# Splitting the first convolution chunk over all four quadrants of the matmul array, with the tap sums formed in PSUM and a weight copied in column halves

## The chip, the cores and the metric

The kernel runs on one core of a Trainium2 chip. A core has a matmul engine (TensorE, PE in the profile) that reads SBUF and writes PSUM, a vector engine (VectorE, DVE), a scalar engine (ScalarE, ACT), a GpSimd engine (POOL, here the issuer of casting loads), a SyncE queue (SP, here the issuer of stores and transposing transfers) and 16 DMA engines. The metric is the device time of one execution in microseconds; lower is better.

## The reference

Two layers in a row. The first is a causal convolution over the sequence, 7 taps, with one softmax-normalised set of taps for each of 8 heads (24 channels each). The second is a two-layer network with a leaky ReLU.

```
x: (8, 4096, 192) f32   weight: (8, 7)   w_in: (192, 2048)   w_out: (2048, 192)
w    = softmax(weight, axis=-1)          # with + 1e-9 in the denominator
conv[b, s, ch] = sum_k w[head(ch), k] * x_padded[b, s + k, ch]    # 6 zeros in front
h    = conv.reshape(32768, 192) @ w_in
out  = maximum(0.01 * h, h) @ w_out
```

## The kernel before

**Tiling.** Channels are cut into 3 chunks (`NCH`) of 64. Two batch rows share the 128 partitions: row e (0 or 1) of a pair has partitions 64e to 64e+63. `xt[pair]` holds x transposed (channels on partitions, tokens along the free side) in bf16, `yt[block]` the convolved block of 512 tokens (`ST`). The first two blocks are cut into halves of 256 tokens, so that `groups` begins with four groups of 256 and goes on with whole blocks. For each group the loop at the end of the kernel runs steps of first-layer matmuls (`mm1`, line 494: `ph` <- `w_in`, `yt`), a leaky ReLU on ScalarE (line 501: `g` <- `ph`) and second-layer matmuls of the group before (lines 511 and 574). The convolution of a later group is made by VectorE (lines 226 and 232: one instruction per chunk and tap).

**The opening.** Before any of that runs, the first group needs its convolution quickly, and there TensorE does it: for each chunk c, part p and tap k it multiplies 256 tokens, shifted by k, with a 64x64 diagonal matrix `diag[c][:, p, k, :]` (line 257, `acc` <- `xt`, `diag`), adding the 14 products in PSUM. The taps are split in two bf16 parts (p = 0 the rounded exponential, p = 1 the remainder), so that no precision is lost; a third part is used only for the sum. Matmuls with 64 rows and 64 columns take one quadrant of the array each: e gives the row half, the output's partitions the column half. With `cross` the output of row e goes to the other half of the partitions, so that a crossed chunk and a straight one use all four quadrants; its evacuation crosses back.

**Order in the opening.** Everything is written out by hand, and each engine takes its instructions in program order.

- The exponentials of the weights (ScalarE, line 370) are split into three bf16 parts on VectorE (lines 377 to 380, `w9p`), and three 48-column matmuls with the 0/1 matrix `sel` spread parts 0 and 1 over the channels (`select`, line 394); VectorE copies them to SBUF as `whm` (line 407).
- TensorE runs warm-up matmuls (line 358) between these pieces. Block 0's first 256 tokens are transposed by matmuls against `ident` (line 179), with a `select` of part 2 in the middle, and copied to `xt` by ScalarE (line 199).
- The diagonals: VectorE makes planes of 7 taps (`diag_wide`, line 413: chunk 0 both parts, chunk 2 part 0, four taps of chunk 1 part 1, chunk 2 part 1), ScalarE single taps (`diag_each`, line 421: the other ten of chunk 1).
- VectorE adds the parts (line 441 `wml`), forms the denominator (line 443) and its reciprocal `rsum` (line 447). Then it copies `w_in[0]` within SBUF (`spread_down` line 320, `spread_up` line 323): each half of the first-layer weights is loaded once and needed on both partition halves.
- TensorE: chunk 0 part 0 alone (7 steps of 2 matmuls), chunk 0 part 1 with chunk 2 part 0 (7 steps of 4), chunk 1 part 1 with chunk 2 part 1 (7 of 4), chunk 1 part 0 alone (7 of 2).
- Evacuations, scaled by `rsum`: chunk 0 on ScalarE (line 452), chunk 2 half on ScalarE and half on VectorE (line 276), chunk 1 on ScalarE.
- TensorE transposes the next 256 tokens from `x_rows[1]` (line 188), which POOL's queue loads; VectorE copies them to `xt` (line 199) and forms `wk`, the normalised taps for its own convolutions (lines 469 and 470).
- The main loop's group 0: chunks in the order 0, 2, 1 (`FIRST`). Behind its first two units TensorE starts the convolution of group 1, chunks 0 and 2 (line 257 again), in three cuts, while VectorE makes chunk 1 of it (seven taps, lines 226 and 232) with the copies of `w_in[1]` behind the third tap. Units 0 and 1 of `mm1` read columns 0 to 511 of `w_in[0]`, units 2 and 3 columns 512 to 1023, units 4 to 7 the same of `w_in[1]`.

PSUM: pool `po` has four one-bank buffers for the transposes and the accumulators, pool `ph` two buffers of two banks; `wa` (warm-ups) and `wps` (the `select` outputs) have the first two turns of `ph`, the first-layer outputs the next.

## Time and profile before

| | us |
|---|---|
| median of 4 runs (lowest, highest) | 681.78 (681.32, 682.85) |
| the profiled execution | 681.65 |
| its span, first to last instruction | 679.9 |
| TensorE busy | 675.9 (99%) |
| VectorE busy | 480.8 (71%) |
| ScalarE busy | 518.7 (76%) |
| first-layer matmuls, line 494, busy | 377.1 |
| second-layer matmuls, line 574, busy | 339.9 |
| convolution matmuls, line 257 (140 of them), busy | 5.5 |
| copies of `w_in`, lines 320 and 323 (4), busy | 2.3 |

Times in a timeline are microseconds from the start of the span; a row merges instructions of one kind that follow each other, "start, length, engine, line, operation, output<-inputs, shape, count", and in brackets the idle time before it with what ended it. Matmuls are pipelined: a row's length holds the latency of its last instruction, so the step from one to the next is found from the count and the mean. A matmul of a pair or a four of quadrants starts a few ns after its neighbour.

### The profile page before, as it was taken

How to read it: one execution, taken by the hardware profiler on the slowest of the kernel's cores; microseconds unless marked ns; L12 is line 12 of the kernel's file. 1: busy time of each engine (PE TensorE's matmuls, PEld its weight loads, DVE VectorE, ACT ScalarE, POOL GpSimd, SP SyncE). 2: the span in 40 equal slices, each digit the busy share in tenths (PEclk: the TensorE clock that was granted, in tenths of full speed). 3: DMA queues.
4: the chain of work that ended last, by engine and by line, in shares of the span. 5: the costliest groups of instructions: out<-in, count | busy, mean ns of one | idle time of the engine just before them, and what ended most of it. 6: DMA issues, size and time to landing. Idle time of an engine off the chain costs nothing.

```text
span 679.9 us, 27088 instructions
## 1 busy us (share of the span) xinstructions
PE 675.9 (99%) x12444; PEld 447.3 (66%) x12444; DVE 480.8 (71%) x811; ACT 518.7 (76%) x608; POOL 146.8 (22%) x205
## 2 busy tenths in 40 slices
PE   9999999999999999999999999999999999999998
PEld 6997666666666666666666666666666666666667
DVE  7989468766768666778667687667786676876612
ACT  7899777777777778777777877778777777777781
POOL 7455210222201222202222202222022220000000
PEclk9999999999999999999999999999999999999999
DMA  9998745656737557456556556667375573321123
GB/s 150 93 111 110 58 79 88 81 63 73 95 72 96 71 56 88 81 86 87 64 65 92 87 84 76 58 83 94 73 90 66 59 95 73 72 56 35 32 50 94
DMA packets 213826, 53.27 MB, mean 78 GB/s; under 512 B 209232, under 2 KB 213328, under 8 KB 213712
## 3 DMA queue, kind: packets, MB, share of 16 engines
q0 software_dynamic: 98752, 13.97, 30.4%
q1 hardware_dynamic: 114944, 37.57, 28.0%
q8 instruction: 97, 1.59, 1.0%
q14 instruction: 17, 0.14, 0.1%
q10 hardware_dynamic: 16, 0.00, 0.0%
HBM read 28.31 MB, written 25.17 MB: 79 GB/s over the span
## 4 chain that ended last, share of the span: by engine, by line
PE 99%; DVE 0%; issue 0%
PE ph L494 49%; PE acc L574 44%; PE po L511 5%; PE acc L257 1%; PE warm L358 1%; PE ptr L188 0%; PE ptr L179 0%; DVE o_sb L622 0%; PE warm L394 0%; PE wps L394 0%
## 5 line engine op out<-in xcount | busy, mean ns | idle before, releaser
L501 ACT ACTIVATE g<-ph 128x1024 bf16<-128x1024 f32 x512 | 496.6, 1021 | 140.3 <-PE ph L494 140.1
L232 DVE SCALAR_TENSOR_TENSOR yt<-xt,wk,yt 128x512 bf16<-128x512 bf16 (+1 forms) x582 | 380.3, 716 | 0.2
L494 PE MATMUL ph<-yt,w_in 64*64 64x512 bf16 (+2 forms) x6048 | 377.1, 369 | 0.0
L574 PE MATMUL acc<-g,w_out 64*64 64x512 bf16 x5568 | 339.9, 376 | 0.0
L494 PEld LDWEIGHTS <-w_in 64*64 64x64 bf16 (+1 forms) x6048 | 229.6, 131 | 102.8 <-issue 0.8
L574 PEld LDWEIGHTS <-w_out 64*64 64x64 bf16 x5568 | 178.2, 118 | 118.8
L99 POOL DMA_DIRECT2D x_bf<-in_x_dram x180 | 134.2, 774 | 410.6 <-DMA xt<-x_bf 408.0
L596 DVE STREAM_TRANSPOSE o_t<-acc 128x512 f32<-128x512 f32 x87 | 72.9, 875 | 181.6 <-PE acc L574 181.6
L511 PE MATMUL po<-w_out,g 64*128 64x192 bf16 (+1 forms) x640 | 36.8, 243 | 0.0
L511 PEld LDWEIGHTS <-g 64*128 64x128 bf16 (+1 forms) x640 | 32.6, 95 | 3.2 <-issue 0.4
L226 DVE TENSOR_SCALAR yt<-xt,wk 128x512 bf16<-128x512 bf16 (+1 forms) x97 | 28.7, 320 | 3.5 <-ACT g L501 3.3
L584 ACT COPY junk<-junk 128x1 f32<-128x1 f32 x58 | 11.1, 191 | 4.1
L622 DVE COPY o_sb<-po 128x192 f32<-128x192 f32 x8 | 2.8, 356 | 6.8 <-PE po L511 4.2
L257 PE MATMUL acc<-xt,diag 64*64 64x256 bf16 x140 | 5.5, 275 | 0.0
L622 ACT COPY o_sb<-po 128x192 f32<-128x192 f32 x16 | 5.1, 323 | 0.3
L257 PEld LDWEIGHTS <-diag 64*64 64x64 bf16 x140 | 4.4, 107 | 1.4 <-DVE diag L413 0.7
L358 PE MATMUL warm<-const-bfloat16-1.0 128*128 128x512 bf16 (+3 forms) x12 | 4.3, 514 | 0.8 <-PEq L734 0.8
L152 POOL DMA_DIRECT2D x_half<-in_x_dram x6 | 4.6, 773 | 1.1 <-DMA w_in<-in_moe_w_in_dram 1.0
L358 PEld LDWEIGHTS <-const-bfloat16-1.0 128*128 128x128 bf16 x12 | 1.5, 138 | 2.5 <-issue 2.5
L148 POOL DMA_DIRECT2D x_rows<-in_x_dram x4 | 2.9, 742 | 0.0
L413 DVE TENSOR_TENSOR diag<-ident,whm 128x448 bf16<-128x448 bf16 (+1 forms) x5 | 2.6, 578 | 0.0
L421 ACT ACTIVATE diag<-ident,whm 128x64 bf16<-128x64 bf16 x10 | 2.5, 335 | 0.0
(47 smaller groups left out, 24.0 us busy)
## 6 DMA issues: line engine op xcount, KB each, us to landing
out_dram<-o_t SPq DMA_DIRECT2D x116, 192.0 KB, 4.6
x_bf<-in_x_dram POOLq DMA_DIRECT2D x180, 64.0 KB, 3.3
out_dram<-o_sb SPq DMA_DIRECT2D x8, 192.0 KB, 3.0
xt<-x_bf SPq DMA_TRANSPOSE x90, 3.9
w_out<-in_moe_w_out_dram POOLq DMA_DIRECT2D x2, 384.0 KB, 8.3
out_dram<-o_sb SPq DMA_DIRECT2D x8, 96.0 KB, 1.9
w_in<-in_moe_w_in_dram POOLq DMA_DIRECT2D x2, 256.0 KB, 5.3
x_nat<-in_x_dram SPq DMA_DIRECT2D x2, 192.0 KB, 2.6
```

The lines of the kernel that those rows point to most:

```text
L99: ins = nc.gpsimd.dma_start(out=t[:, c, :, e, :], in_=src[2 * rp + e, :, :, c * CH : (c + 1) * CH],)
L226: lambda s=src, d=dst, c=c: nc.vector.tensor_scalar_mul(d, s, wk[:, c, 0:1])
L232: lambda s=src, d=dst, c=c, k=k: nc.vector.scalar_tensor_tensor(out=d, in0=s, scalar=wk[:, c, k : k + 1], in1=d, op0=mybir.AluOpType.mult, ...
L257: lambda k=k, p=p, a=a, ps=ps, to=to, acc=accs[e * apart]: nc.tensor.matmul(out=acc[to, :T], lhsT=diag[c][ps, p, k, :], rhs=xt[0][ps, c, a ...
L358: nc.tensor.matmul(out=wa[:, 0, 0:cols], lhsT=ones[:, 0:128], rhs=ones[:, 0:cols], start=True, stop=True,)
L494: nc.tensor.matmul(out=ph[m : m + M, e, i * T : (i + 1) * T], lhsT=w_in_of(f, e, c, m, m + M), rhs=y[ps, c, t0 : t0 + T], start=(c == chun ...
L501: act = nc.scalar.activation(out=g[blk][:, nf * u : nf * (u + 1), :, t0 : t0 + T], in_=ph.rearrange("p e (i t) -> p i e t", i=nf), func=my ...
L511: return nc.tensor.matmul(out=po[m], lhsT=g[b][ps, fc, e, s * 128 : (s + 1) * 128], rhs=w_out[ps, fc, :], start=start, stop=stop,)
L574: ins = nc.tensor.matmul(out=acc2[gi, r][e * CH : (e + 1) * CH, 0:T], lhsT=w_out_of(ps, fc, r), rhs=g[b][ps, fc, e, t0 : t0 + T], start=fi ...
L584: seal = nc.scalar.copy(out=junk, in_=junk)
L596: nc.vector.transpose(out=osb[gi, 0][:, 0 : T // GB, :, r], in_=acc2.pop((gi, r))[:, 0:T].rearrange("p (j k) -> p j k", k=GB),)
L622: ins = copy(out=o_sb[:, n % 2, :], in_=po.pop(n))
```

## The change

- Chunk 0 (`pe_conv_quads`): the 256 tokens are cut in two halves of 128. For each part and tap four matmuls run: the first half of the tokens straight into `acc0`, the second half crossed into the second bank of `wps`. That is 56 matmuls of 128 columns where there were 28 of 256. The first half is evacuated by ScalarE, the second by two VectorE instructions that cross back (64 partitions x 128).
- Chunks 1 and 2 now run together, 14 steps of four. Chunk 1's taps have the order `late`: ScalarE's three of part 1, VectorE's four of part 1, then part 0.
- The sum of the tap parts moves from VectorE to PSUM: `select` adds four parts (three and a constant 1e-9 for the denominator) in twelve 48-column matmuls behind the first transposes, in place of three in the middle of them and of a 512-column warm-up; a 192-column warm-up takes the place in the middle. VectorE forms the reciprocal and `wk` directly from PSUM, ahead of the copies.
- The copies of `w_in` are cut by column halves (`spread(n, h)`). For `w_in[0]` the first half stands behind chunk 0's evacuation and ahead of chunk 2's, the second behind the transposes of the next 256 tokens and ahead of their copies to `xt`. For `w_in[1]` the halves stand around VectorE's fourth tap.

```diff
--- before.py
+++ after.py
@@ -236,7 +236,7 @@
                 )
         return jobs
 
-    def pe_conv_jobs(grp, c, parts=(0, 1), cross=False, apart=False):
+    def pe_conv_jobs(grp, c, taps=None, cross=False, apart=False):
 
 
 
@@ -246,22 +246,22 @@
             for i in range(2 if apart else 1)
         ]
         jobs = []
-        for p in parts:
-            for k in range(K):
-                a = BASE + k + blk * ST + t0
-                both = []
-                for e in range(2):
-                    ps = slice(e * CH, (e + 1) * CH)
-                    to = slice((e ^ cross) * CH, ((e ^ cross) + 1) * CH)
-                    both.append(
-                        lambda k=k, p=p, a=a, ps=ps, to=to, acc=accs[e * apart]: nc.tensor.matmul(
-                            out=acc[to, :T], lhsT=diag[c][ps, p, k, :],
-                            rhs=xt[0][ps, c, a : a + T],
-                            start=(k == 0 and p == parts[0]),
-                            stop=(k == K - 1 and p == parts[1]),
-                        )
+        taps = taps or [(p, k) for p in range(2) for k in range(K)]
+        for p, k in taps:
+            a = BASE + k + blk * ST + t0
+            both = []
+            for e in range(2):
+                ps = slice(e * CH, (e + 1) * CH)
+                to = slice((e ^ cross) * CH, ((e ^ cross) + 1) * CH)
+                both.append(
+                    lambda k=k, p=p, a=a, ps=ps, to=to, acc=accs[e * apart]: nc.tensor.matmul(
+                        out=acc[to, :T], lhsT=diag[c][ps, p, k, :],
+                        rhs=xt[0][ps, c, a : a + T],
+                        start=((p, k) == taps[0]),
+                        stop=((p, k) == taps[-1]),
                     )
-                jobs.append(both)
+                )
+            jobs.append(both)
 
         def evac(*scale):
             if blk not in yt:
@@ -277,6 +277,43 @@
 
         return jobs, evac
 
+    def pe_conv_quads(grp, c, other):
+
+
+        blk, t0, T = grp
+        n = T // 2
+        accs = [psum_o.tile([128, ST], FP32, name="acc0", tag="po"), other]
+        jobs = []
+        for p in range(2):
+            for k in range(K):
+                a = BASE + k + blk * ST + t0
+                four = []
+                for h in range(2):
+                    for e in range(2):
+                        ps = slice(e * CH, (e + 1) * CH)
+                        to = slice((e ^ h) * CH, ((e ^ h) + 1) * CH)
+                        four.append(
+                            lambda k=k, p=p, a=a + h * n, ps=ps, to=to, acc=accs[h]: nc.tensor.matmul(
+                                out=acc[to, :n], lhsT=diag[c][ps, p, k, :],
+                                rhs=xt[0][ps, c, a : a + n],
+                                start=(k == 0 and p == 0),
+                                stop=(k == K - 1 and p == 1),
+                            )
+                        )
+                jobs.append(four)
+
+        def evac(straight, crossed):
+            if blk not in yt:
+                yt[blk] = yt_pool.tile([128, NCH, ST], BF16, name="yt")
+            y = yt[blk][:, c, t0 : t0 + T]
+            straight(y[:, 0:n], accs[0][:, :n], rsum[:, c, :])
+            for e in range(2):
+                ps = slice(e * CH, (e + 1) * CH)
+                frm = slice((1 - e) * CH, (2 - e) * CH)
+                crossed(y[ps, n:T], accs[1][frm, :n], rsum[frm, c, :])
+
+        return jobs, evac
+
     def run(*lists):
         for slots in zip_longest(*lists, fillvalue=()):
             for both in slots:
@@ -291,8 +328,9 @@
     ones = nc.const_aps.tensor(1.0, [128, ST], BF16)
     junk = const_pool.tile([128, 1], FP32)
     nc.vector.memset(junk, 0.0)
-    w9p = const_pool.tile([128, 3, K + 1], BF16, name="w9p")
+    w9p = const_pool.tile([128, 4, K + 1], BF16, name="w9p")
     nc.vector.memset(w9p, 0.0)
+    nc.vector.memset(w9p[:, 3, K:], 1e-9)
 
     sel = const_pool.tile([128, NCH, 2, CH], BF16, name="sel")
     nc.gpsimd.memset(sel[:, :, 0, :], 1.0)
@@ -316,11 +354,12 @@
             in_=moe_w_in[rows : rows + ps[1], n * WF : (n + 1) * WF],
         )
 
-    def spread_down(n):
-        nc.vector.tensor_copy(out=w_in[n][0:CH, 1, :], in_=w_in[n][CH:128, 0, :])
-
-    def spread_up(n):
-        nc.vector.tensor_copy(out=w_in[n][CH:128, 1:3, :], in_=w_in[n][0:CH, 0:3:2, :])
+    def spread(n, h):
+        cols = slice(h * WF // 2, (h + 1) * WF // 2)
+        nc.vector.tensor_copy(
+            out=w_in[n][CH:128, 1:3, cols], in_=w_in[n][0:CH, 0:3:2, cols]
+        )
+        nc.vector.tensor_copy(out=w_in[n][0:CH, 1, cols], in_=w_in[n][CH:128, 0, cols])
 
     def w_in_of(f, e, c, m0, m1):
         n, f = divmod(f, NFC // NPW)
@@ -385,17 +424,19 @@
     warm(3, 128)
     wps = psum_h.tile([128, 2, ST], FP32, name="wps", tag="ph")
     wps_hm = wps[:, 0, 0 : NCH * FILL].rearrange("p (c r q k) -> p c r q k", c=NCH, q=2, k=K + 1)
-    wps_l = wa[:, 1, 0 : NCH * FILL].rearrange("p (c r q k) -> p c r q k", c=NCH, q=1, k=K + 1)
-
-    def select(out, parts):
-        q = parts.stop - parts.start
-        r = FILL // (q * (K + 1))
+    wsum = wa[:, 1, 0 : NCH * FILL].rearrange("p (c r q k) -> p c r q k", c=NCH, q=1, k=K + 1)
+
+    def select(out, *parts):
         for c in range(NCH):
-            nc.tensor.matmul(
-                out=out[:, c], lhsT=sel[:, c].rearrange("p e k -> p (e k)"),
-                rhs=w9p[:, None, parts, :].to_broadcast([128, r, q, K + 1]),
-                start=True, stop=True,
-            )
+            for i, part in enumerate(parts):
+                q = part.stop - part.start
+                nc.tensor.matmul(
+                    out=out[:, c], lhsT=sel[:, c].rearrange("p e k -> p (e k)"),
+                    rhs=w9p[:, None, part, :].to_broadcast(
+                        [128, FILL // (q * (K + 1)), q, K + 1]
+                    ),
+                    start=(i == 0), stop=(i == len(parts) - 1),
+                )
 
     select(wps_hm, slice(0, 2))
     wps_hm = wps_hm[:, :, 0]
@@ -425,9 +466,9 @@
 
 
     warm(1, 192)
-    transpose_first(0, lambda: select(wps_l, slice(2, 3)))
-    wps_l = wps_l[:, :, 0, 0]
-    warm(1, ST)
+    transpose_first(0, lambda: warm(1, 192))
+    select(wsum, *(slice(i, i + 1) for i in range(4)))
+    wsum = wsum[:, :, 0, 0]
     warm(1, 384)
     evac_first(0, nc.scalar.copy, nc.scalar.copy)
     for p in range(2):
@@ -437,37 +478,29 @@
     diag_wide(2, 1, K)
     diag_each(1, 1, range(VK, K))
     diag_each(1, 0, range(K))
-    wml = const_pool.tile([128, NCH, K + 1], FP32, name="wml")
-    nc.vector.tensor_add(wml, wps_l, whm[:, :, 1])
     rsum = const_pool.tile([128, NCH, 1], FP32)
-    nc.vector.scalar_tensor_tensor(
-        out=rsum, in0=wml[:, :, K:], scalar=1e-9, in1=whm[:, :, 0, K:],
-        op0=mybir.AluOpType.add, op1=mybir.AluOpType.add,
-    )
-    nc.vector.reciprocal(rsum, rsum)
-    spread_down(0)
-    spread_up(0)
+    nc.vector.reciprocal(rsum, wsum[:, :, K:])
+    wk = const_pool.tile([128, NCH, K], FP32, name="wk")
+    nc.vector.tensor_mul(wk, wsum[:, :, 0:K], rsum.to_broadcast([128, NCH, K]))
 
     def act_scale(out, in_, scale):
         nc.scalar.activation(
             out=out, in_=in_, func=mybir.ActivationFunctionType.Copy, scale=scale
         )
 
-    pe_0, evac_0 = pe_conv_jobs(groups[0], 0)
+    pe_0, evac_0 = pe_conv_quads(groups[0], 0, wps[:, 1, :])
     pe_2, evac_2 = pe_conv_jobs(groups[0], 2, cross=True, apart=True)
-    pe_1, evac_1 = pe_conv_jobs(groups[0], 1, (1, 0))
-    run(pe_0[:K])
-    run(pe_0[K:], pe_2[:K])
-    evac_0(act_scale)
-    run(pe_1[:K], pe_2[K:])
-    run(pe_1[K:])
+    late = [(1, k) for k in (*range(VK, K), *range(VK))] + [(0, k) for k in range(K)]
+    pe_1, evac_1 = pe_conv_jobs(groups[0], 1, late)
+    run(pe_0)
+    run(pe_1, pe_2)
+    evac_0(act_scale, nc.vector.tensor_scalar_mul)
+    spread(0, 0)
     evac_2(act_scale, nc.vector.tensor_scalar_mul)
     evac_1(act_scale)
     transpose_first(1)
+    spread(0, 1)
     evac_first(1, nc.vector.tensor_copy, nc.vector.tensor_copy)
-    wk = const_pool.tile([128, NCH, K], FP32, name="wk")
-    nc.vector.tensor_add(wk, whm[:, :, 0, 0:K], wml[:, :, 0:K])
-    nc.vector.tensor_mul(wk, wk, rsum.to_broadcast([128, NCH, K]))
 
 
     g, po, acc2, osb, seal = {}, {}, {}, {}, None
@@ -672,9 +705,10 @@
                     conv_1 = conv_jobs(groups[1], (1,))
                     for job in conv_1[:3]:
                         job()
-                    spread_down(1)
-                    spread_up(1)
-                    for job in conv_1[3:]:
+                    spread(1, 0)
+                    conv_1[3]()
+                    spread(1, 1)
+                    for job in conv_1[4:]:
                         job()
                     pe_0, evac_0 = pe_conv_jobs(groups[1], 0)
                     pe_2, evac_2 = pe_conv_jobs(groups[1], 2, cross=True)
```

## The prediction

> **What bounds the kernel now.** I read the page first (busy shares, then the chain that ended last), then the timeline of each engine over the first 20 us, because the change touches nothing later, then the transfers that feed that stretch, then the place where VectorE's later backlog meets TensorE.
>
> ```profile
> PE 99%; DVE 0%; issue 0%
> ```
>
> The chain that ended last is TensorE for 99% of the span. From 17 us to the end I found no pause between matmuls beyond the 0.1 us of a change of tile shape. So a time won or lost on TensorE in the opening reaches the end one for one, and nothing can be won behind the opening.
>
> TensorE's timeline in the opening (start, length, line, count):
>
> ```profile
> 4.74 0.95 PE L358 MATMUL warm<-const-bfloat16-1.0 128*128 128x512 bf16 x2
> 5.63 3.40 PE L257 MATMUL acc<-xt,diag 64*64 64x256 bf16 x84
> 8.96 0.53 PE L188 MATMUL ptr<-ident,x_rows 128*64 128x128 bf16 x12
> 9.41 1.50 PE L494 MATMUL ph<-yt,w_in 64*128 64x256 bf16 x24
> 10.85 0.85 PE L257 MATMUL acc<-xt,diag 64*64 64x256 bf16 x24
> ```
>
> The 84 matmuls of the first convolution are 28 steps (7 of two, 14 of four, 7 of two). The point to watch is 10.85: there the second half's convolution starts, which needs `xt` from VectorE. VectorE and ScalarE beside it:
>
> ```profile
> 6.96 0.17 DVE L441 TENSOR_TENSOR wml<-warm,whm 128x24 f32<-128x24 f32 x1
> 7.16 0.16 DVE L443 SCALAR_TENSOR_TENSOR rsum<-wml,whm 128x3 f32<-128x3 f32 x1
> 7.36 0.18 DVE L447 RECIPROCAL rsum<-rsum 128x3 f32<-128x3 f32 x1
> 7.57 0.42 DVE L320 COPY w_in<-w_in 64x1024 bf16<-64x1024 bf16 x1
> 8.02 0.77 DVE L323 COPY w_in<-w_in 64x2048 bf16<-64x2048 bf16 x1
> 8.71 0.46 DVE L276 TENSOR_SCALAR yt<-acc,rsum 64x256 bf16<-64x256 f32 x1
> 9.53 0.62 DVE L199 COPY xt<-ptr 128x384 bf16<-128x384 bf16 x2 [0.35 <-PE ptr L188]
> 10.06 0.17 DVE L469 TENSOR_TENSOR wk<-whm,wml 128x21 f32<-128x21 f32 x1
> 10.27 0.18 DVE L470 TENSOR_TENSOR wk<-wk,rsum 128x21 f32<-128x21 f32 x1
> 10.56 0.29 DVE L226 TENSOR_SCALAR yt<-xt,wk 128x256 bf16<-128x256 bf16 x1
> ```
>
> ```profile
> 5.36 2.49 ACT L421 ACTIVATE diag<-ident,whm 128x64 bf16<-128x64 bf16 x10
> 7.75 1.02 ACT L452 ACTIVATE yt<-acc,rsum 128x256 bf16<-128x256 f32 x2
> 9.07 0.48 ACT L452 ACTIVATE yt<-acc,rsum 128x256 bf16<-128x256 f32 x1 [0.29 <-PE acc L257]
> ```
>
> VectorE has no idle from 4.47 to 9.17, and the copies of `w_in` fill its wait for the convolution. Its `xt` copies end at 10.15, 0.70 before TensorE wants them. ScalarE's first evacuation starts only when its ten `diag` instructions are through. Last, the transposes' source; this is the answer for the two loads of `x_rows` issued at 3.60 and 4.31:
>
> ```profile
> DMA to landing us min/median/max: 4.3/4.3/4.4
> ```
>
> They land at about 8.0 and 8.6.
>
> **The change part by part.** *Before the convolution.* TensorE loses three 48-column matmuls and a 512-column warm-up (0.43 from 4.74 to the next) and gains a 192-column one in place of the three (0.16, what they took) and twelve of 48 columns. Three of those lay at 4.28, 4.35 and 4.39, so twelve take 0.51, between 0.04 and 0.07 each (0.48 and 0.84). The convolution starts 0.08 later, at 5.71 (5.68 to 6.04). The first `diag` plane (0.63 from 4.47) and `xt` (done 5.47) are there by then.
>
> *Chunk 0.* Fourteen steps of two matmuls become fourteen steps of four with half the columns. No row has four tiles of 128 columns. The transposes in row 8.96 have 128 columns in two tiles: twelve in 0.53, less the 0.22 of the last, over five steps, is 0.06 a step (0.055 by their starts). The four-tile steps of 256 columns in row 10.85 give (0.85-0.27)/5 = 0.116. These are the ends; I take 0.055, since four tiles of 256 columns cost no more there than two do (24 matmuls in 12 steps of row 9.41 also have 0.11).
>
> One thing has to be added: TensorE is at half rate at first. The nine warm-ups from 0.84 (3,456 columns in 2.84 us) run at 1.2 columns per ns against 2.35 later, and the convolution's first pairs lie at 5.63, 5.84, 6.01 and 6.12, so the rate doubled at about 5.97, although the granted clock reads 1.00 throughout. With 2.4 steps at 0.107 and 11.6 at 0.055, chunk 0 ends issuing at 6.61. Its second plane of `diag` (done 5.63) is in time.
>
> [...]
>
> *Chunks 1 and 2 together*: 14 steps of four at 0.109, 6.61 to 8.14, where they ended at 8.87 before. Every tap's `diag` is in time: ScalarE's last ends at 7.85 and is used at 8.03, VectorE's last at 7.04 and is used at 7.37. So the convolution is 0.73 shorter. If steps of four cost 0.11, nothing is won and it ends at 8.9.
>
> *What is late next.* The transposes cannot follow at 8.24, because `x_rows` lands at 8.56 (the later of the two): they start at 8.62, a gain of 0.34 instead of 0.73, and the first-layer matmuls could start at 9.08. TensorE's queue stands behind that wait. This is the floor of the change: -0.34.
>
> *VectorE.* Removed: two small additions (0.20 each, start to start) before 7.57, and 0.5 behind the `xt` copies (10.06 to 10.56). Added: the reciprocal at 6.96, the product `wk` at 7.16, then at 7.36 two crossed evacuations of 64x128. A 64x256 one lasts 0.46 and takes 0.51 in sequence (two in 1.00 at 16.37); the 128x48 copy `whm` lasts 0.20. So 1.28 ns a column: 0.35 each in sequence, between 0.20 and 0.51. They end at 8.06. Then the first column half of `w_in`: 64x1024 is 0.45 (7.57 to 8.02), and from 1024 to 2048 columns costs 0.24 more (8.02 to 8.71), so 64x512 is 0.33, together 0.78 (0.57 if halves cost half the wholes' 1.14, 0.90 if 512 columns cost as much as 1024). It ends at 8.84. Only then comes VectorE's part of chunk 2, though TensorE has been ready since 8.3: 8.84 to 9.30. Chunk 2 is second in the first-layer order, so TensorE, having started at 9.08, stands at it until 9.37, against 9.55 before. ScalarE gives chunk 1 at 9.2 (its two evacuations follow each other from 8.33), in time. Second column half: 9.35 to 10.13. Only behind it the two `xt` copies (0.62): 10.75, and with 0.06 for the semaphore TensorE's convolution starts at 10.81. TensorE itself would be there at 9.37+1.30 = 10.67. **So 10.85 becomes 10.81: -0.04.** The reserve of 0.70 that the `xt` copies had is what pays for the longer VectorE chain: +0.7 for crossed evacuations, +0.42 for the copies in four pieces, -0.2 for the additions.
>
> *Behind it.* `wk` is ready early, so VectorE's first tap starts at 10.85 instead of 10.56. The four pieces of the second `w_in` take 1.56 instead of 1.17 (11.92 to 13.09), so its seven taps end at 15.85 instead of 15.14. Before, VectorE idled 0.71 there until 15.85 for TensorE; that cover is now spent, and used up to nothing. The halves are ready at 13.0 and 14.3, before TensorE's 13.74 and 15.75. From then on VectorE runs without idle until its backlog ends:
>
> ```profile
> 43.55 2.73 DVE L232 SCALAR_TENSOR_TENSOR yt<-xt,wk,yt 128x512 bf16<-128x512 bf16 x4
> ...
> 46.58 0.81 PE L494 MATMUL ph<-yt,w_in 64*128 64x512 bf16 x6
> ```
>
> It ends at 46.28, and the matmuls that read it start at 46.58 (the chunk written last 0.22 later), so a slip of VectorE of up to 0.3 costs nothing there. POOL's and SP's queues keep their order. The zeroing and the 1e-9 fill at 0.9 lie in VectorE's 0.97 of idle: nothing, and 0.07 without it.
>
> Sum: 681.65 of the profiled execution (span 679.9, 1.75 around it) - 0.04 = **681.6**; the median of the four runs, 681.78, lies 0.13 above that execution, and the runs differ by 1.5.
> Bounds: -0.34 (VectorE at its cheap ends, `x_rows` decides) to VectorE at its dear ends, 7.36+1.02+0.90+0.51+0.90+0.62+0.06 = 11.37, +0.52.
>
> **Rivals.** *VectorE's pieces are cheap*: `x_rows` decides, the full 0.34 comes through, 681.3. For it: VectorE's independent instructions overlap (the two `xt` copies of 0.35 each take 0.62). Against: the evacuations at 16.37 do not.
>
> *VectorE becomes the bound outright*: dear ends, 682.2; it costs as soon as its part up to the `xt` copies exceeds 3.45 us from 7.36. This one also slips the taps, but the 0.3 at 46.28 takes most of that.
>
> *The array does not take four 128-column matmuls at once* (that the change does nothing): steps of 0.11, convolution to 8.9, chunk 2 from VectorE at 9.6, then 0.78 and 0.62: 11.1, +0.27, 681.9.
>
> *The slower side: the rate doubles later.* The last work before the convolution is now twelve tiny matmuls instead of a 512-column one. If the half rate lasted through the convolution, 14 steps of 0.107 and 14 of 0.213 would end at 10.19; VectorE's chunk 2 then starts at 10.41, its copies end at 12.32, the second convolution starts at 12.38: +1.53, 683.2. It decides once the convolution ends later than about 10.0, where it costs 1.36. Against: 48 columns at 0.04 keep the array streaming.
> [...]
>
> **How the numbers follow.** A difference of 0.2%, 1.36 us, is about what a measurement of this kernel tells from no change. Forecast 0.55, cheap pieces 0.13, dear VectorE 0.12, no quadrant gain 0.06, later rate 0.09, something unseen 0.05. Only the later rate passes 1.36, so slower is 0.11 with part of the unseen. No case reaches -1.36; 0.05 for faster is the unseen. Same: 0.84. The range runs from the floor less half the spread of the runs to the dear end plus it: 680.9 to 682.8.
>
> **What would show it.** Chunk 0 as 56 matmuls of 128 columns over about 0.9 us; transposes near 8.6, not 8.2; a pause of 0.3 in the first-layer matmuls at chunk 2; the second convolution at 10.5 to 11.4 released by VectorE's `xt` copy; no idle of VectorE before 15.85. Wrong if VectorE's copies are much dearer beside the DMA issues, if the rate doubles at another time, or if VectorE's lost reserve shows again at 46 us.

## The result, and the profile after

The changed kernel takes 682.27 us (median of 41 runs, 682.06 to 684.82) against 681.66 us for the kernel before (median of 61 runs on the same chips, 681.31 to 682.85). The ratio is 1.001, with a 95% interval of 1.0005 to 1.0014. So it is slower by 0.6 us, 0.1%: less than the 0.2% that I named as the bound of "no change", yet with this many runs the interval leaves 1 out. I had forecast 0.04 less. The profiled execution of the changed kernel took 682.89 (span 681.2), 0.62 above its own median; before it was 681.65 (span 679.9). That extra 0.62 fits a late transfer, which stands below; one profiled execution cannot show it.

The chain that ended last is no longer TensorE for 99% of the span. This is its line in the page of the changed kernel:

```profile
PE 97%; DMA 1%; POOL 1%; DVE 0%; issue 0%; POOLq 0%; DVEq 0%
```

The chain now leaves TensorE in the opening and goes back through VectorE's copy of the second `w_in` to its transfer (1% of the span, 5.57 to 13.05 us) and POOL, which issued it. TensorE's timeline in the opening of the changed kernel (start, length, line, operation, count; in brackets the idle time in front and who ended it):

```profile
5.75 0.31 PE L296 MATMUL acc<-xt,diag 64*64 64x128 bf16 x2
...
6.45 0.21 PE L296 MATMUL acc<-xt,diag 64*64 64x128 bf16 x2
6.51 0.22 PE L296 MATMUL acc<-xt,diag 64*64 64x128 bf16 x2
...
8.37 0.24 PE L188 MATMUL ptr<-ident,x_rows 128*64 128x128 bf16 x1
8.87 0.52 PE L188 MATMUL ptr<-ident,x_rows 128*64 128x128 bf16 x11 [0.26 <-DMA x_rows<-in_x_dram]
9.32 0.40 PE L527 MATMUL ph<-yt,w_in 64*128 64x256 bf16 x3
9.99 1.39 PE L527 MATMUL ph<-yt,w_in 64*128 64x256 bf16 x21 [0.27 <-DVE w_in L359]
11.31 0.85 PE L257 MATMUL acc<-xt,diag 64*64 64x256 bf16 x24
12.10 1.57 PE L527 MATMUL ph<-yt,w_in 64*128 64x256 bf16 x24
13.60 0.74 PE L257 MATMUL acc<-xt,diag 64*64 64x256 bf16 x20
14.27 0.41 PE L527 MATMUL ph<-yt,w_in 64*128 64x256 bf16 x3
15.15 1.39 PE L527 MATMUL ph<-yt,w_in 64*128 64x256 bf16 x21 [0.48 <-DVE w_in L359]
```

L296 is the line of the new four-quadrant matmuls; L257 is still the convolution, L188 the transposes, L527 the first layer (L494 before). The reader is to see three things. The four-quadrant steps follow each other by 0.055 (6.45 to 6.51), and the last matmul of the convolution starts at 8.17 instead of 8.76. The transposes then wait for `x_rows`. And the first layer stops twice after three matmuls, at 9.6 and at 14.5, both times for a copy at L359: that is the upward copy of `spread`, the one that writes rows 1 and 2 of `w_in` on partitions 64 to 127. The second convolution starts at 11.31, where it was 10.85.

The waits of the same kernel from 5 to 20 us (total us, times, longest) say it once more; the weight loads (PEld) are what waits, the matmuls behind them (PE) only show the rest:

```profile
PEld L527 <- DVE w_in L359: 1.3, 2, 0.7
PE ph L527 <- DVE w_in L359: 0.7, 2, 0.5
DVE w_in L359 <- DMA w_in<-in_moe_w_in_dram: 0.7, 1, 0.7
```

VectorE in the changed kernel:

```profile
7.37 0.73 DVE L313 TENSOR_SCALAR yt<-wps,rsum 64x128 bf16<-64x128 f32 x2
8.03 0.50 DVE L359 COPY w_in<-w_in 64x1024 bf16<-64x1024 bf16 x1
8.56 0.54 DVE L362 COPY w_in<-w_in 64x512 bf16<-64x512 bf16 x1
9.11 0.48 DVE L276 TENSOR_SCALAR yt<-acc,rsum 64x256 bf16<-64x256 f32 x1
9.51 0.42 DVE L359 COPY w_in<-w_in 64x1024 bf16<-64x1024 bf16 x1
9.96 0.54 DVE L362 COPY w_in<-w_in 64x512 bf16<-64x512 bf16 x1
10.43 0.60 DVE L199 COPY xt<-ptr 128x384 bf16<-128x384 bf16 x2
...
13.14 0.42 DVE L359 COPY w_in<-w_in 64x1024 bf16<-64x1024 bf16 x1 [0.68 <-DMA w_in<-in_moe_w_in_dram]
13.60 0.53 DVE L362 COPY w_in<-w_in 64x512 bf16<-64x512 bf16 x1
14.68 0.42 DVE L359 COPY w_in<-w_in 64x1024 bf16<-64x1024 bf16 x1
```

TensorE resumes at 9.99, and what ends just before is not the evacuation of chunk 2 (9.11 + 0.48 = 9.59) but the upward copy of the *second* column half (9.51 + 0.42 = 9.93). At 15.15 it is the same: 14.68 + 0.42 = 15.10. Yet the unit that stands there reads columns 0 to 511 alone. The wait is put in when the program is built, from the stretch of addresses that each instruction covers from its first to its last element: that is my reading, and the rows bear it out. The upward copy writes columns 512 to 1023 of rows 1 and 2; from the first of these to the last lie columns 0 to 511 of row 2, which the weight load reads. So the two are ordered though they share no element. The three matmuls that pass tell this from an ordering by whole tiles or whole rows: the second of them reads columns 0 to 511 of row 1 on the same partitions 64 to 127, in the same tile and in a row that the copy also writes, but ahead of the copy's first address, and it runs at once; the fourth, the first that stands, reads row 2. In this execution the second `w_in` also landed late: VectorE waited 0.68 for it at 13.14, and with it the later pause grew.

POOL issues loads through the whole first stretch of copies:

```profile
7.51 1.47 POOL L385 DMA_DIRECT2D w_out<-in_moe_w_out_dram  x2
8.90 1.49 POOL L152 DMA_DIRECT2D x_half<-in_x_dram  x2
```

### The profile page after: what moved, and what is told of

It is laid out like the page before. It is cut to its first block, busy times and chain, and to the rows that moved or that the text cites. A ratio compares the mean times of both kernels' runs of the same rounds, so it can differ in the third digit from the quotient of the medians.

```text
span 681.2 us, 27167 instructions
## 1 busy us (share of the span) xinstructions
PE 676.1 (99%) x12481; PEld 446.6 (66%) x12481; DVE 482.2 (71%) x815; ACT 518.6 (76%) x608; POOL 146.1 (21%) x205
## 4 chain that ended last, share of the span: by engine, by line
PE 97%; DMA 1%; POOL 1%; DVE 0%; issue 0%; POOLq 0%; DVEq 0%
PE ph L527 48%; PE acc L607 44%; PE po L544 5%; DMA w_in<-in_moe_w_in_dram 1%; POOL w_in L352 0%; POOL x_rows L148 0%; DVE w_in L359 0%; POOL sel L338 0%; DVE w_in L362 0%; DVE yt L232 0%; PE ptr L188 0%; PE acc L257 0%; DVE o_sb L655 0%; POOL ident masks.py:199 0%; POOL sel L336 0%
## 5 line engine op out<-in xcount | busy, mean ns | idle before, releaser
L527 PE MATMUL ph<-yt,w_in 64*64 64x512 bf16 (+2 forms) x6048 | 377.7, 369 | 0.7 <-DVE w_in L359 0.7
L527 PEld LDWEIGHTS <-w_in 64*64 64x64 bf16 (+1 forms) x6048 | 229.0, 131 | 104.7 <-DVE w_in L359 1.3
L226 DVE TENSOR_SCALAR yt<-xt,wk 128x512 bf16<-128x512 bf16 (+1 forms) x97 | 30.1, 339 | 2.4 <-PE ph L527 1.2
L257 PE MATMUL acc<-xt,diag 64*64 64x256 bf16 x112 | 3.8, 271 | 0.0
L257 PEld LDWEIGHTS <-diag 64*64 64x64 bf16 x112 | 2.8, 106 | 0.6 <-issue 0.6
```

The source lines that it names most:

```text
L226: lambda s=src, d=dst, c=c: nc.vector.tensor_scalar_mul(d, s, wk[:, c, 0:1])
L257: lambda k=k, p=p, a=a, ps=ps, to=to, acc=accs[e * apart]: nc.tensor.matmul(out=acc[to, :T], lhsT=diag[c][ps, p, k, :], rhs=xt[0][ps, c, a ...
L527: nc.tensor.matmul(out=ph[m : m + M, e, i * T : (i + 1) * T], lhsT=w_in_of(f, e, c, m, m + M), rhs=y[ps, c, t0 : t0 + T], start=(c == chun ...
```

## The experiments

My theory after the result: (A) half of the loss is the wait for the wrong half, and (B) the other half is a VectorE chain that is longer than I made it, because its copies last longer beside POOL's loads. The rivals: (C) the copies in halves cost more in themselves, whatever the waits; (D) the quadrants or the sums in PSUM cost something; (E) the opening is bound by the landing of `x_rows` and no order of VectorE's work matters. "Before" below is always the kernel before in runs on the same chip. Each timed version has 11 runs, and the 95% interval of its ratio to the kernel before is 0.0009 wide to either side, 0.6 us, as much as the whole loss. Differences of 0.2 to 0.4 between medians are therefore read together with the timelines. What stands by the runs alone is this: none of the 41 runs of the changed kernel was below 682.06, and of the versions below, 6 of 11 (`own_tile`), 7 (`quiet_changed`) and 8 (`own_quiet`) were.

**Copies into tiles of their own.** The matmuls read the copied rows from one tile per half, so no span reaches over another half's columns; all else as in the changed kernel.

```diff
-        nc.vector.tensor_copy(
-            out=w_in[n][CH:128, 1:3, cols], in_=w_in[n][0:CH, 0:3:2, cols]
-        )
-        nc.vector.tensor_copy(out=w_in[n][0:CH, 1, cols], in_=w_in[n][CH:128, 0, cols])
+        nc.vector.tensor_copy(out=w_sp[n][h][CH:128], in_=w_in[n][0:CH, 0:3:2, cols])
+        nc.vector.tensor_copy(out=w_sp[n][h][0:CH, 0], in_=w_in[n][CH:128, 0, cols])
```

> The changed kernel, with the copies of w_in written to tiles of their own (one per column half) instead of the middle of w_in; number, size and order of all instructions stay. Theory A (chunk 2's weight load on partitions 64 to 127 waits for the second half's upward copy, because that copy's rows 1 and 2 span the place that it reads): the wait on the copy goes; chunk 2 then follows VectorE's evacuation, at about 9.65 instead of 9.99 in the profile, and the pause at the fifth unit (14.4 to 15.15) goes as well; the second convolution starts at about 11.1, held by the xt copies, instead of 11.31; time 681.8 to 682.0. Theory B (VectorE is only longer, the wait on the copy is a symptom): the second convolution stays at 11.3 and the time at 682.2 to 682.3.

Measured: 681.89 (681.84 to 682.62, 11 runs; before 681.69), ratio 1.0005, interval 0.9996 to 1.0014. TensorE's timeline:

```profile
9.66 0.30 PE L535 MATMUL ph<-yt,w_sp 64*128 64x256 bf16 x2 [0.54 <-DVE yt L276]
...
11.08 0.85 PE L257 MATMUL acc<-xt,diag 64*64 64x256 bf16 x24
```

The first layer now goes on at 9.66, right behind VectorE's evacuation, and it does not stop at the fifth unit. So (A) is a true part: in medians 0.38 of the 0.61. But the second convolution is still 0.23 later than before, which (A) alone does not explain.

**No halves.** The four quadrants and the sums as in the change, but `w_in` copied whole, downward first, at the place of the first half.

```diff
-    def spread(n, h):
-        cols = slice(h * WF // 2, (h + 1) * WF // 2)
...
+    def spread(n):
+        nc.vector.tensor_copy(out=w_in[n][0:CH, 1, :], in_=w_in[n][CH:128, 0, :])
+        nc.vector.tensor_copy(out=w_in[n][CH:128, 1:3, :], in_=w_in[n][0:CH, 0:3:2, :])
```

> The changed kernel with whole copies of w_in (one down, one up) where the first column half stood, none later: quadrants and PSUM sums stay, column halves go. Theory A: no weight load waits on a later copy; VectorE's chunk 2 runs from about 9.2 to 9.66 and the xt copies end at 10.3, so chunk 2 is read at 9.72 and the second convolution starts at 11.0; about 681.8. If the quadrants or the PSUM sums cost the time, it stays at 682.2 or more.

Measured: 682.00 (681.99 to 682.15; before 681.69), 0.2 above what I expected. VectorE and TensorE show why:

```profile
8.55 0.94 DVE L359 COPY w_in<-w_in 64x2048 bf16<-64x2048 bf16 x1
9.41 0.46 DVE L276 TENSOR_SCALAR yt<-acc,rsum 64x256 bf16<-64x256 f32 x1
```

```profile
9.55 1.74 PE L523 MATMUL ph<-yt,w_in 64*128 64x256 bf16 x23 [0.63 <-DVE w_in L359]
11.22 0.85 PE L257 MATMUL acc<-xt,diag 64*64 64x256 bf16 x24
```

The large copy lasted 0.94; in the kernel before it took 0.77. TensorE stands for that copy until 9.55 and then for the evacuation behind it, which ends at 9.87; the `xt` copies are done at 10.53, well ahead of 11.22. So VectorE's work up to the evacuation of chunk 2 decides here. This speaks against (C) as the whole cause: without halves the median is still 0.3 above the kernel before.

**Halves alone**, on the kernel before: its convolution and its additions stay, only the four copies stand where the change puts them.

```diff
-    spread_down(0)
-    spread_up(0)
+    spread(0, 0)
...
     transpose_first(1)
+    spread(0, 1)
     evac_first(1, nc.vector.tensor_copy, nc.vector.tensor_copy)
```

> The kernel before with only the column halves, at the changed kernel's places. Theory A: chunk 2 waits for the second half's upward copy, at about 9.6 (+0.1), and the fifth unit for that of the second w_in (+0.3 to 0.5): 682.0 to 682.2, most of the whole change's loss without its other parts. If the halves are harmless: 681.6 to 681.8.

Measured: 681.96 (681.78 to 682.72; before 681.69). TensorE, and the first copy on VectorE, in its profiled execution, which was the dearest of its runs (682.72):

```profile
9.99 1.39 PE L495 MATMUL ph<-yt,w_in 64*128 64x256 bf16 x21 [0.35 <-DVE w_in L321]
11.31 0.85 PE L257 MATMUL acc<-xt,diag 64*64 64x256 bf16 x24
...
14.94 1.39 PE L495 MATMUL ph<-yt,w_in 64*128 64x256 bf16 x21 [0.33 <-DVE w_in L321]
```

```profile
7.77 0.75 DVE L321 COPY w_in<-w_in 64x1024 bf16<-64x1024 bf16 x1 [0.32 <-DMA w_in<-in_moe_w_in_dram]
```

Both pauses come with the halves alone, so they need no quadrants. That they fall in the same places as in the changed kernel is chance: here VectorE has no crossed evacuations, but it waited 0.32 for the first `w_in` and its first copy lasted 0.75, so that the second began at 8.55, against 8.56 there. The median is 0.31 below the changed kernel's: how much the wait costs depends on how long VectorE's chain is, and the crossed evacuations lengthen that by 0.66.

**Sums in PSUM alone**, on the kernel before: the four-part `select`, and `rsum` and `wk` from it.

```diff
-    wml = const_pool.tile([128, NCH, K + 1], FP32, name="wml")
-    nc.vector.tensor_add(wml, wps_l, whm[:, :, 1])
...
+    nc.vector.reciprocal(rsum, wsum[:, :, K:])
+    nc.vector.tensor_mul(wk, wsum[:, :, 0:K], rsum.to_broadcast([128, NCH, K]))
```

> The kernel before with only the tap sums moved into PSUM (four parts in twelve small matmuls, reciprocal and normalised taps straight from PSUM ahead of the copies). TensorE's convolution starts 0.08 later, VectorE has 0.2 less before the copies and 0.5 less behind the xt copies, where nothing waits: same time as before within 0.1, 681.6 to 681.8. If the small matmuls put off the doubling of the matmul rate, it is slower by 0.3 or more.

Measured: 681.59 (681.34 to 682.57; before 681.60), ratio 1.0000. VectorE reaches its first copy at 7.33 instead of 7.57 and later waits 0.42 for the transposes. In this run the sums cost nothing: (D) falls for this part.

**Less on VectorE.** Whole copies, and one of the two crossed evacuations on ScalarE (`crossed[e]` with a list of two).

```diff
-    evac_0(act_scale, nc.vector.tensor_scalar_mul)
+    evac_0(act_scale, nc.vector.tensor_scalar_mul, act_scale)
```

> As whole_copies, and one of the two crossed evacuations of chunk 0 given to ScalarE. Theory A with VectorE as what is late next: VectorE's chunk 2 runs from about 8.9 to 9.4, ScalarE's chunk 1 ends at 9.45, so chunks 2 and 1 are read at 9.43 and 9.54 without a pause; the second convolution starts at 10.7 against 10.85 before: 681.5, faster than both kernels. If x_rows or something else sets the end, no better than whole_copies.

Measured: 681.68 (681.42 to 682.14; before 681.69), ratio 1.0001, interval 0.9992 to 1.0009; I had hoped for 681.5. TensorE's timeline:

```profile
8.86 0.52 PE L188 MATMUL ptr<-ident,x_rows 128*64 128x128 bf16 x11 [0.27 <-DMA x_rows<-in_x_dram]
9.31 1.53 PE L523 MATMUL ph<-yt,w_in 64*128 64x256 bf16 x24
10.77 0.85 PE L257 MATMUL acc<-xt,diag 64*64 64x256 bf16 x24
11.56 1.77 PE L523 MATMUL ph<-yt,w_in 64*128 64x256 bf16 x24
```

The first layer runs through (1.53 for its 24 matmuls). Against `whole_copies`, which differs by that one evacuation, VectorE's first copy starts 0.49 sooner (7.57 against 8.06), its two copies lasted 0.21 less, and the second convolution starts 0.45 sooner (10.77 against 11.22): VectorE's chain is what counts. The gain on the kernel before, 0.08 at 10.77, is lost again in the next row: 1.77 instead of the 1.51 of `whole_copies`, with a pause of 0.34 at about 12.5 in which TensorE waits for nothing that the profile shows.

**The wait for `x_rows` taken out.** On the kernel just shown, the second 256 tokens are transposed from `x_half`, which is there long before, so their convolution is computed from the wrong tokens.

```diff
-                        in_=x_rows[q][:, e, s, c * CH : (c + 1) * CH],
+                        in_=(
+                            x_half[0][:, c, s, e, :] if q == 1
+                            else x_rows[q][:, e, s, c * CH : (c + 1) * CH]
+                        ),
```

> shared_evac, with the second 256 tokens transposed from the first block's data, which is there already, instead of x_rows: their convolution is left wrong, the work stays. It takes the wait for the x_rows load out of TensorE's queue. If x_rows is what keeps the shorter convolution from showing: the transposes start at 8.2 to 8.3 instead of 8.9, but chunk 2 still comes from VectorE at about 9.4, so the second convolution gains 0.1 at most (10.65 to 10.75) and the time is 681.5 to 681.7. If x_rows alone were the limit, the first-layer matmuls would start at 8.7 and the time would fall by 0.4 against shared_evac, to 681.2 to 681.3.

Measured: 681.65 (681.41 to 682.66; before 681.60). TensorE:

```profile
8.19 0.53 PE L188 MATMUL ptr<-ident,x_half 128*64 128x128 bf16 x12
8.64 2.21 PE L526 MATMUL ph<-yt,w_in 64*128 64x256 bf16 x24
10.79 0.85 PE L260 MATMUL acc<-xt,diag 64*64 64x256 bf16 x24
```

The first layer starts 0.67 sooner (8.64 against 9.31) and the second convolution does not: 10.79. The first layer takes 2.21 instead of 1.53: its matmuls of chunk 2 go on at 9.36, behind VectorE's evacuation (it ends at 9.31), and those of chunk 1 at 9.57, behind ScalarE's (9.51). (E) falls: behind the wait for `x_rows` stands a second one of the same length. `own_second` below says the same for the changed kernel's order: there `x_rows` was in time by chance and the transposes were through by 8.55, yet the second convolution starts at 11.31, as in the changed kernel.

**Own tile for one `w_in` only**, the first (`own_first`) or the second (`own_second`).

```diff
+        up = w_sp[h][CH:128] if n else w_in[n][CH:128, 1:3, cols]
+        down = w_sp[h][0:CH, 0] if n else w_in[n][0:CH, 1, cols]
```

> The changed kernel with tiles of their own for the copies of the first w_in alone; the second w_in keeps the wait. It splits the two pauses. Theory A: chunk 2 of the first unit is read at about 9.65, the second convolution starts at 11.1, as in own_tile; at the fifth unit the wait on the second upward copy stays, where VectorE is by then about 0.2 earlier than in the changed kernel: 0.1 to 0.5 there. Time between own_tile (681.89) and the changed kernel (682.27): 681.9 to 682.15.

> The changed kernel with tiles of their own for the copies of the second w_in alone; the first w_in keeps its wait. If the wait at the fifth unit is worth the 0.38 of own_tile by itself: no pause there, but the second convolution stays at 11.3 (0.2 later than in own_tile), so 681.9 to 682.15. If the two waits are worth 0.2 each and add up: 682.05 to 682.1; own_first then should not have stayed at 682.26.

Measured: `own_first` 682.26 (681.99 to 682.57; before 681.60), `own_second` 682.09 (ten of eleven runs 682.07 to 682.11, one 683.02; before 681.58). TensorE of the first, then of the second:

```profile
11.07 0.85 PE L257 MATMUL acc<-xt,diag 64*64 64x256 bf16 x24
13.98 0.41 PE L534 MATMUL ph<-yt,w_in 64*128 64x256 bf16 x3
14.75 1.39 PE L534 MATMUL ph<-yt,w_in 64*128 64x256 bf16 x21 [0.37 <-DVE w_in L363]
```

```profile
9.98 1.39 PE L534 MATMUL ph<-yt,w_in 64*128 64x256 bf16 x21 [1.10 <-DVE w_in L363]
11.31 0.85 PE L257 MATMUL acc<-xt,diag 64*64 64x256 bf16 x24
```

Taking only the first wait away gains nothing (682.26 against 682.27; I had expected 681.9 to 682.15): TensorE starts the fifth unit 0.29 sooner (13.98 against 14.27) and stands in it for VectorE's later copy, whose chain does not start sooner (VectorE's first tap is at 11.13 in both). Taking only the later one away gains 0.18, and both 0.38. The 682.07 to 682.11 of `own_second` is also where 15 of the 41 runs of the changed kernel lie (682.06 to 682.15). That fits runs in which the later wait costs nothing, and others in which the second `w_in` lands later, as in the profiled execution; with one profiled execution this is not shown.

**POOL quiet during the copies.** In the changed kernel the loads of `w_out` and `x` that POOL issues from 7.5 us are moved behind the last copy of the first `w_in`.

```diff
-    for h in range(2):
-        cs = ...
-        nc.gpsimd.dma_start(out=w_out...)
-    load_first(3)
-    load_x(2)
...
-    spread(0, 1)
+    last_copy = spread(0, 1)
     evac_first(1, nc.vector.tensor_copy, nc.vector.tensor_copy)
+    for h in range(2):
+        ins = nc.gpsimd.dma_start(out=w_out...)
+        if h == 0:
+            sync(ins, last_copy, "POOL quiet while w_in is copied")
+    load_first(3)
+    load_x(2)
```

> The changed kernel with POOL's loads of w_out and all that follow them held until the copies of the first w_in are done: a look at the four copies with no load being issued beside them. If the issuing of loads is what makes a 64x512 copy take 0.53 instead of 0.29, the four copies take 0.42, 0.29, 0.42, 0.29. If 512 columns are slow by themselves, the short ones stay at 0.53. The time is of no interest: w_out lands 2 us later than the second layer wants it.

Measured: 681.84 in its one execution. VectorE in it:

```profile
7.98 0.41 DVE L359 COPY w_in<-w_in 64x1024 bf16<-64x1024 bf16 x1
8.42 0.29 DVE L362 COPY w_in<-w_in 64x512 bf16<-64x512 bf16 x1
8.72 0.48 DVE L276 TENSOR_SCALAR yt<-acc,rsum 64x256 bf16<-64x256 f32 x1
9.13 0.41 DVE L359 COPY w_in<-w_in 64x1024 bf16<-64x1024 bf16 x1
9.57 0.29 DVE L362 COPY w_in<-w_in 64x512 bf16<-64x512 bf16 x1
```

The copies last 0.41, 0.29, 0.41 and 0.29, against 0.50, 0.54, 0.42 and 0.54 beside the loads; the evacuation, which reads PSUM, lasts 0.48 in both. That is (B): 0.60 of VectorE's time in the four copies. It is the issuing on POOL and not the transfers: from the first copy to the last the DMA engines moved 180 GB/s here (7.98 to 9.86) and 159 in the changed kernel (8.03 to 10.50). The same kernel run again for its time:

> The kernel of pool_quiet once more, timed: the changed kernel with POOL's loads of w_out and what follows held until the first w_in is copied. If the stretching of VectorE's copies by POOL's loads is a part of the loss beside the wait on the later copy: chunk 2 at 9.6 instead of 9.99, second convolution at 10.9 instead of 11.3, 681.8 to 682.0. If the wait alone is the loss, the time stays at 682.2.

Measured: 681.88 (681.81 to 682.60; before 681.70). The second convolution starts at 10.94, and the pause at the fifth unit is 0.17. Its control, the same hold put into the kernel before:

> The kernel before with the same hold on POOL, as the control for shared_quiet: its VectorE has 0.7 in reserve at the xt copies and its TensorE reaches the 449th record at 14.2, so nothing should move: 681.5 to 681.7. If it falls as far as shared_quiet, the hold is the gain, not the quadrants.

Measured: 681.71 (681.31 to 682.23; before 681.70), so no cost or gain of later loads by themselves is to be seen.

**Both causes removed**: own tiles and POOL quiet.

> own_tile with POOL's loads of w_out and what follows held until the first w_in is copied. If the stretched copies are what is left of the loss: copies of 0.41 and 0.29, chunk 2 at 9.35 to 9.6, second convolution at 10.75 to 10.9, no pause at the fifth unit, 681.6 to 681.75, the time of the kernel before. If something else is left (quadrants, crossed evacuations), it stays at 681.85 to 681.9.

Measured: 681.62 (681.31 to 682.82; before 681.58), ratio 1.0003, interval 0.9994 to 1.0012. TensorE:

```profile
8.35 0.53 PE L188 MATMUL ptr<-ident,x_rows 128*64 128x128 bf16 x12
...
10.71 0.85 PE L257 MATMUL acc<-xt,diag 64*64 64x256 bf16 x24
```

In the median the whole loss is gone, with the quadrants, the sums and the halves all in place; the interval alone would still allow 0.8, but eight of the eleven runs are below every run of the changed kernel. The halves do cost VectorE time in themselves (1.40 for four copies, against 0.42 + 0.69 for the two whole ones), but with POOL quiet that time is covered. (C) and (D) fall as causes of the loss by themselves, though both draw on VectorE's reserve. Nothing is won either, though the second convolution starts 0.14 sooner than before.

**Attempts at a gain.** The kernel with one crossed evacuation on ScalarE, with POOL quiet as well:

> shared_evac with the same hold on POOL. Two effects are looked for: copies of 0.42 and 0.69, so that VectorE's part of chunk 2 ends at about 9.2; and the 16 KB of instructions, which TensorE waited for at its 449th record in shared_evac (0.34) and no_rows_wait (0.58), land earlier when fewer loads are on the DMA engines: no pause there. Expected 681.3 to 681.5, faster than the kernel before by 0.1 to 0.3. If the opening is bound by x_rows and the evacuations alone: 681.6 to 681.7.

Measured: 681.91 (681.33 to 682.15; before 681.70), ratio 1.0000, interval 0.9991 to 1.0009: no gain, against 681.3 to 681.5 expected. The second convolution came at 10.67, the earliest of all, and TensorE did not pause at 12.5; but VectorE had to wait for the transfer itself:

```profile
12.43 0.42 DVE L358 COPY w_in<-w_in 64x1024 bf16<-64x1024 bf16 x1 [0.84 <-DMA w_in<-in_moe_w_in_dram]
```

In this execution the second `w_in` is the next thing that is late. The last one asks about the pause of TensorE at 12.5. It comes behind TensorE's 449th record (matmuls and weight loads together). A 16 KB transfer on the instruction queue ended at 11.43 in `shared_evac` and at 11.79 in `no_rows_wait`, 1.4 and 1.3 before TensorE went on; in `shared_quiet` and `own_quiet`, which come to that record just as early (12.37 and 12.39) and do not pause, it ended at 10.94 and 10.78. Here the six opening warm-ups became 48 short ones, so that this record comes earlier.

```diff
-    warm(6, ST)
+    warm(48, ST // 8)
```

> shared_evac with the six 512-column warm-ups cut into 48 of 64 columns: the same columns, 84 more TensorE records ahead of the convolution. If TensorE has to wait for its instructions at the 449th record, that record now comes 84 records earlier in the work, at about 10.5 to 11, and the pause there grows to 1 to 2 us unless the transfer starts earlier too. If the pause in shared_evac has another cause, it stays near 12.5 with 0.3 and the time stays at 681.4 to 682.2.

Measured: 681.95 (one execution). The record came at 10.73, without a pause, but the transfer was earlier too, so this tells nothing apart. What TensorE waits for at 12.5 stays open; that it is this transfer, as I put it beforehand, is not shown.

## Why the prediction was wrong, point by point

**The quadrants (right).** Start of the convolution 5.71, measured 5.75. Steps of four at 0.055: measured 0.055, once the rate had doubled at about 6.1. The end of the issue at 8.14: the last step starts at 8.16, so by its 0.11 the issue ends at 8.27. The two quadrants that stood idle beside a pair do take their matmuls: in the kernel before a pair of 256 columns stepped by 0.108 (7.99 to 8.10), here four of 256 step by 0.109 and four of 128 by 0.055.

**"x_rows lands at 8.56 … the transposes start at 8.62" (right in kind).** The last piece, issued at 4.31, landed 4.5 later, at 8.8, and eleven of the twelve transposes stand until 8.87, 0.25 later. That they, and not the convolution, set the floor was right; `no_rows_wait` shows that the evacuations make a floor of the same height.

**Crossed evacuations (right).** 0.35 each, the next instruction at 8.06: measured 8.03.

**"64x512 is 0.33, together 0.78" (the size was off).** One column half took 1.08, 8.03 to 9.11: the 64x512 copy lasted 0.54, with 0.55 to the next. I gave 0.90 as the dear end. The price of 0.33 came from the difference between rows that themselves lay beside POOL's loads; with POOL quiet the copy lasts 0.29 (`pool_quiet`), so the estimate was near for a quiet POOL and wrong for the POOL of this kernel. I had named "VectorE's copies are much dearer beside the DMA issues" as what would make me wrong, and had not costed it. The rows show what it touches: the copy from SBUF to SBUF took 0.29 in `pool_quiet` and 0.54 here, the evacuation, which reads PSUM, 0.48 in both. The instructions that issue a load last 0.7 each on POOL (two of `w_out` in 1.47 from 7.51), and no copy lost as much: 0.34 at most (a 64x1024 copy of 0.75 in `halves_only`, 0.41 in `pool_quiet`), and some lost nothing. By what means the issuing stretches a copy no run shows.

**"TensorE … stands at it until 9.37" (the step that failed).** It stood until 9.99. I had taken the first-layer units in chunk 2 to wait for VectorE's evacuation and for their own column half. They waited for the second half as well (its upward copy ends at 9.93, they go on at 9.99): by the reading above, the ordering goes by stretches of addresses and not by elements. And the second upward copy stands *behind* the evacuation on VectorE. By my own prices the evacuation ended at 9.30 and that copy (0.45 from 9.35) at 9.80; with 0.06 for the semaphore (9.93 to 9.99) and the 1.32 that the remaining 21 matmuls took (9.99 to 11.31) the second convolution would have come at 11.18. So this step alone turns the sign: +0.33 where I forecast -0.04. The same assumption is in "The halves are ready at 13.0 and 14.3, before TensorE's 13.74 and 15.75": the fifth unit needs both halves, at 15.10 in the profiled execution, and TensorE was there at 14.41.

**"10.85 becomes 10.81" (wrong through these two).** 11.31. Without the false wait 11.08 (`own_tile`), without the disturbed copies 10.94 (`quiet_changed`), without both 10.71 (`own_quiet`), 0.10 under my value. In medians: 682.27, 681.89, 681.88 and 681.62. The two causes are not simply added, since each hides part of the other: VectorE's `xt` copies stand behind the same four copies.

**"The reserve of 0.70 … pays" (overdrawn).** My three items come to 0.92, more than 0.70; the sum held only because VectorE also idled 0.35 ahead of its `xt` copies, 1.05 in all. The two column halves drew 2.00 from VectorE (1.08 and 0.92) instead of 1.56, and the `xt` copies ended at 11.03. That alone puts the second convolution at 11.08, 0.23 late, as `own_tile` has it: this mis-sized term turns the sign by itself, too.

**Behind 17 us (right).** There is no new pause; and VectorE's backlog, which runs without idle past 46 us, holds TensorE up nowhere.

**The rivals.** The nearest was "VectorE becomes the bound outright", at 682.2, to which I gave 0.12; its condition (VectorE's part up to the `xt` copies over 3.45 from 7.36) was met: 7.37 to 11.03 is 3.66, and its half of the loss is shown. The false wait was in no rival. "The array does not take four matmuls at once" and "pieces are cheap" are refuted by the first two timelines. "The rate doubles later" did not come: the doubling was at about 6.1 here, against 5.97, and at 6.7 at the latest in any run (`more_instr`). My "although the granted clock reads 1.00 throughout" took the view for more than it holds; the last section has what the trace holds.

Why no version beats the kernel before is shown as far as this: with VectorE relieved the second convolution starts at 10.67 to 10.79 instead of 10.85, and three other things are late within the next 0.3: `x_rows` and the evacuations at the first layer (`no_rows_wait`), and the landing of the second `w_in` (`shared_quiet`). The fourth, the pause at 12.5 in `shared_evac` and `no_rows_wait`, is seen and not explained.

## What to carry to other kernels

When a copy is split so that a reader can start on its first part, look at the address span of each part, not only at its elements: here the reader of one part waited for the last part of a strided tile whose parts interleave in memory, wherever that now stood in its engine's queue (9.99 instead of 9.66 with tiles of their own), which I read as an ordering by address span. Price an instruction from a row with the same neighbours: a SBUF-to-SBUF copy on VectorE beside loads that POOL issues took here up to nearly twice the same copy alone (64x512: 0.57 in `own_tile` against 0.29 in `pool_quiet`). And when one bound is removed from an opening in which several engines end within a few tenths, count what ends next before counting the gain.

## What the runs showed of the hardware that I had not expected

- VectorE's copies from SBUF to SBUF lasted longer in many places beside loads issued by POOL: 64x512 bf16 0.29 alone (`pool_quiet`) and 0.29 to 0.57 (`own_tile`) beside them, 64x1024 0.41 and up to 0.75 (`halves_only`), 64x2048 0.69 (`before_quiet`) and up to 0.97 (`more_instr`). Not every overlap does it: with POOL issuing for the whole time a 64x512 copy still took 0.29 in `own_second` (at 12.94) and in `halves_only` (at 14.92), and a 64x2048 copy 0.69 in the kernel before (at 12.37). What tells the overlaps apart stays open. VectorE's first tap (line 226, also from SBUF to SBUF) lasts 0.29 alone (10.56 in the kernel before) and up to 0.54 (`halves_only`). Evacuations from PSUM did not change (0.46 to 0.49 for 64x256).
- When the matmul rate doubles is not fixed: the first matmuls at the full rate lie at 6.01 before, at 6.17 in the changed kernel and at 4.27 in `own_tile`. The views give the granted clock as 1.00 throughout, but the trace holds a record of it only from 5.96, 6.14 and 4.25 on, just where the spacing of the matmuls halves; before that it holds none, and the views count that as 1.00. Over the kernels here (`own_quiet` has no such record) it begins between 3.57 (`own_second`) and 6.64 (`more_instr`). The convolution starts at 5.12 or at 5.71 accordingly (`own_tile`, `own_first`), and the second convolution is at 11.08 and 11.07: the 0.6 is absorbed where VectorE sets the pace. Two of these kernels also repeat far more closely (`own_second` within 0.04 in ten of eleven runs, `whole_copies` within 0.16) than the kernel before (681.31 to 682.85). That the doubling makes that scatter was not tried.
- TensorE pauses 0.34 and 0.58 at about 12.5 in `shared_evac` and `no_rows_wait`, for nothing that the profile shows, and not in `shared_quiet` and `own_quiet`, which come there as early.
